# Feed-forward layers in three token blocks of 768, 384-column matmuls, one shared buffer for three sums of x

## Chip, cores and metric

The kernel runs on one core of a Trainium2 chip. The metric is the device time of one execution in microseconds (us). A core has TensorE (PE in the profile; PEld is its weight load), VectorE (DVE), ScalarE (ACT), GpSimd (POOL), and SyncE (SP), whose queue issues nearly all of this kernel's DMAs. Matmuls write the accumulator memory PSUM, the other engines work in the on-chip memory SBUF.

## What is computed

```python
scores = scale * q @ k^T                      # 4 batches, 8 heads, 576 tokens, 64 wide, causal
local = softmax(scores) @ v
mem_out = (phi(q) @ M_prev) / (phi(q) @ z_prev + 1e-6)
x = g * mem_out + (1 - g) * local             # 2304 tokens x 512
x = mish(x @ moe_w_in) @ moe_w_out            # 512 -> 2048 -> 512
out = silu(x @ moe2_w_in) @ moe2_w_out        # 512 -> 2048 -> 512
```

All is to float32 precision. The four weight matrices come as 64-bit floats and are turned into 32-bit ones on the chip.

## The kernel before

The attention stands first: 16 pairs of heads, each a list of some 70 steps (`pair_steps`, `Attn.steps`). Its result is left in SBUF as `xT`, features down the partitions and the 2304 tokens along. Then come two feed-forward layers (class `Moe`), phases 0 and 1.

A layer is cut into four groups of hidden columns (`NG`) and into token blocks. Before, there are four blocks of 512, 640, 512 and 640 tokens (`TBS` holds half of each, 256 and 320). One pass of a block through a group is a visit (`VISITS`): 32 visits in all. In odd groups the blocks are gone through backwards, so that the last block of a group is the first of the next.

The first product of a visit, x times w_in, is done as a 2 x 2 block product with seven instead of eight multiplications (`PRODUCTS`; numbered 1, 2, 6, 7, 5, 3, 4). Four of the seven take sums of x, called T1 to T4, three take parts of x itself (11, 21, 22). Each operand is split into a high and a low part (ACT rounds the high one, L984, DVE subtracts to get the low one, L977), so that a product is six matmuls of half a block's tokens (`product`, L1013 to L1015). A visit does this for two pairs of hidden chunks (c is 0 or 1): 84 matmuls. They go to the PSUM banks psX, psW and psY. ACT copies a bank out (L1044), DVE adds another to it (L1042), ACT applies Mish or Silu and rounds (L1048 to L1053), DVE takes the low part (L1054); the result is the tile `g`.

The second product, g times w_out (`out_part`, L1081), accumulates in the banks `acc`. In phase 0 the tokens are the columns: 512 of them in the small blocks, 320 twice in the large ones (`cuts`). In phase 1 a matmul always has the 512 output features as its columns. DVE adds `acc` to `xT` (L1102, ACT copies in the first group, L1100).

The split operands of x (seven tiles a block) are kept in two sets of buffers, one for even blocks and one for odd ones (`xop`: `tp % 2`). When a set goes to another block, the tiles are written to device memory once (`spill`, L991) and read back for later groups (`reload`, L995), on SP's queue.

The order in which every engine's instructions stand is computed when the kernel is built: `Steps.plan` plays all steps against a small table of durations and takes, on each engine, the ready step with the earliest due time. `SHIFT` adds a number to the due time of each class of steps; these numbers were sought by trial. A tile or a bank is handed on by `hold`: the first step of the next user waits for the last ones of the user before.

```python
for kc in range(2):
    nc.tensor.matmul(o, lhsT=W(0, kc), rhs=X(0, kc), ...)
    nc.tensor.matmul(o, lhsT=W(0, kc), rhs=X(1, kc), ...)
    nc.tensor.matmul(o, lhsT=W(1, kc), rhs=X(0, kc), ...)
```

Of the kernel before, what the change touches and what calls it, by code (L numbers as in the profile page):

```python
# [342 lines left out]
class Attn:  # L343
# [372 lines left out]
    def register(self, m):  # L716
# [8 lines left out]
        for p in range(B * NP):  # L725
# [213 lines left out]
class Moe:  # L939
    def __init__(self, tc, ctx, xT, weights, out):  # L940
        self.tc, self.nc, self.ctx = tc, tc.nc, ctx
        self.xT, self.w, self.out = xT, weights, out
        self.ps, self.pool = {}, {}
        self.dram = ctx.enter_context(tc.tile_pool(name="spill", bufs=1, space=bass.MemoryType.DRAM))
        self.x, self.g, self.sn, self.bank, self.acc, self.spilled = [{}, {}], {}, {}, {}, {}, {}

    def open(self, n):
# [23 lines left out]
    def splits(self, tp):
# [6 lines left out]
        home = {"T1": "11", "T3": "12", "T2": "22", "T4": "21"}  # L978
# [4 lines left out]
        for x in XOPS:  # L983
            f["h" + x] = lambda x=x: nc.scalar.copy(self.wide(tp, x, 0), B(home.get(x, x)))  # L984
            f["l" + x] = lambda x=x: sub(self.wide(tp, x, 1), B(home.get(x, x)), self.wide(tp, x, 0).bitcast(F32))
        return f

    def spill(self, ph, tp, x):
        t = self.x[tp % 2][x]
        d = self.spilled[ph, tp, x] = self.dram.tile([P, 4 * TBS[tp]], F32, name=f"sp{ph}{tp}{x}")  # L990
        self.nc.sync.dma_start(d, t.rearrange("p h n -> p (h n)").bitcast(F32))  # L991

    def reload(self, ph, tp, x):
        t = self.x[tp % 2][x]
        self.nc.sync.dma_start(t.rearrange("p h n -> p (h n)").bitcast(F32), self.spilled[ph, tp, x])  # L995

    def product(self, q, n):
# [13 lines left out]
        X = lambda h, kc: self.xop(tp, b, h)[:, kc * tb:(kc + 1) * tb]  # L1011
# [5 lines left out]
    def gt(self, q, c):  # L1017
        u = (q, c)
        if u not in self.g:
            k = (2 * (2 * q[0] + q[1]) + c) % 6  # L1020
            self.g[u] = self.pool[0 if k < 2 else 1].tile([P, 2, WIDE], F32R, tag=f"g{k}", name=f"g{k}")
        return self.g[u]

    def vt(self, q, c, h=None):
# [3 lines left out]
        tb = TBS[VISITS[q[0]][2]]  # L1028
        return self.sn[u][:, :2 * tb] if h is None else self.sn[u][:, h * tb:(h + 1) * tb]

    def fin(self, q):
        nc = self.nc
        ph, g, tp = VISITS[q[0]]
        tb = TBS[tp]
# [16 lines left out]
        hi = lambda c: self.gt(q, c)[:, 0, :2 * tb]  # L1051
        for c in range(2):
            f[f"h{c}"] = lambda c=c: nc.scalar.copy(hi(c), val(c))  # L1053
            f[f"l{c}"] = lambda c=c: nc.vector.tensor_tensor(  # L1054
                self.gt(q, c)[:, 1, :2 * tb], val(c), hi(c).bitcast(F32), op=ALU.subtract)
        return f

    def out_part(self, v, d, c):
        nc = self.nc
        ph, g, tp = VISITS[v]  # L1060
        tb = TBS[tp]
# [4 lines left out]
        for j in range(2):  # L1066
            w = self.w.W2[ph, g * GC + 2 * c + j]
            t = self.g[(v, c), j]
            if ph == 0:
                kc, hf = d  # L1070
                n = cuts(v)[0]
# [12 lines left out]
    def part(self, v, d):  # L1084
        ph, g, tp = VISITS[v]
        t0, tb = START[tp], TBS[tp]
        if ph == 0:
            n = cuts(v)[0]
# [3 lines left out]
        return self.xT[:, :, t0 + DM:t0 + DM + P]  # L1092

    def drain(self, v, d):
# [3 lines left out]
        acc = acc[:, :cuts(v)[0]] if ph == 0 else acc if d < KC else acc.rearrange("p (c n) -> p c n", c=KC)  # L1098
# [10 lines left out]
    def register(self, m, base, ends):  # L1109
        V = len(VISITS)  # L1110
        outs = lambda v: [(kc, h) for h in range(2 * TBS[VISITS[v][2]] // cuts(v)[0]) for kc in range(KC)] if (
            VISITS[v][0] == 0) else list(range(2 * TBS[VISITS[v][2]] // P))
        tb = lambda v: TBS[VISITS[v][2]]
        Q = lambda v, c, x: ("Q", (v, c), x)
        O = lambda v, d, c: ("O", (v, c), d)
        od = lambda v: 6 * sum(ff(n) for n in cuts(v))
        pd = lambda v: 6 * ff(tb(v))
# [3 lines left out]
        for v in range(V + 1):  # L1121
            for c in range(2):
# [14 lines left out]
        live = {}  # L1137
        run = []
        for v, (ph, g, tp) in enumerate(VISITS):
            b = tp % 2  # L1140
            if live.get(b, (None,))[0] != (ph, tp):
                live[b] = ((ph, tp), len(run))
                run.append([(ph, tp), [v], "comp" if g == 0 else "load"])
            else:
                run[live[b][1]][1].append(v)
        loaded = {r[0] for r in run if r[2] == "load"}
        ready = {}
        for n, ((ph, tp), vs, kind) in enumerate(run):
            b = tp % 2
            w = 2 * TBS[tp]  # L1150
            K = lambda x: ("X", (n, kind, ph, tp), x)
            users = {x: [Q(v, c, i) for v in vs for c in range(2) for i in PRODUCTS if PRODUCTS[i][1] == x] for x in XOPS}
            need = {x: due[Q(vs[0], 0, i)] for i in PRODUCTS for x in [PRODUCTS[i][1]]}
            if kind == "comp":
                f = self.splits(tp)
                pre = [f"open{b}"]
                if ph == 0:
                    t0 = START[tp]
                    pre += [(bb * NP + kc, e) for bb in range(t0 // S, (t0 + w - 1) // S + 1)
                            for kc in range(NP) for e in ends]  # L1160
                else:
                    pv = VISITS.index((0, NG - 1, tp))
                    pre += [("D", pv, d) for d in outs(pv)]
                D2, A1 = dve(w), sb1(w)
                mk = lambda x, e, d, deps, at: m.add(K(x), e, d, deps, f[x], at - 2.0)
                m.lock.update(K(x) for x in ["l" + x for x in XOPS] + ["T1", "T2", "T3", "T4"])
                mk("T1", "D", D2, [K("l11")], min(need["T1"], need["T2"]))
                mk("T3", "D", D2, [K("T1")], need["T3"])
                mk("T2", "D", D2, [K("T1"), K("T3"), K("l22")], need["T2"])
                mk("T4", "D", D2, [K("T2"), K("l21")], need["T4"])  # L1170
                for x in XOPS:
                    mk("h" + x, "A", A1, [K(x)] if x[0] == "T" else pre, need[x])
                    mk("l" + x, "D", D2, [K("h" + x)], need[x])
                    ready[n, x] = K("l" + x)
                firsts = {x: [K("h" + x)] for x in XOPS}
            else:
                for x in XOPS:
                    m.add(K(x), "S", w * 8 * P / 250e3 + 0.1, [("X", (spill[ph, tp], "comp", ph, tp), "sp" + x)],
                          lambda ph=ph, tp=tp, x=x: self.reload(ph, tp, x), need[x] - 4.0, lag=1.8)
                    ready[n, x] = K(x)  # L1180
                firsts = {x: [K(x)] for x in XOPS}
            lasts = dict(users)
            if kind == "comp" and (ph, tp) in loaded:
                if n == 0:
                    spill = {}
                spill[ph, tp] = n
                for x in XOPS:
                    m.add(K("sp" + x), "S", w * 8 * P / 250e3 + 0.1, [ready[n, x]],
                          lambda ph=ph, tp=tp, x=x: self.spill(ph, tp, x), need[x] + 20.0, lag=1.8)
                    lasts[x] = users[x] + [K("sp" + x)]  # L1190
            for x in XOPS:
                m.cap[f"X.{b}{x}"] = 1
                m.hold(f"X.{b}{x}", n, firsts[x], lasts[x], order=n)
            for v in vs:
                ready[v] = n
# [4 lines left out]
        for v, (ph, g, tp) in enumerate(VISITS):  # L1200
            w = TBS[tp]
            for c in range(2):
# [15 lines left out]
                gd = [f"open{int((2 * (2 * v + c) + j) % 6 >= 2)}" for j in range(2)]  # L1218
                for x, en, d, deps in (
# [4 lines left out]
                        ("h0", "A", sb1(2 * w), [N("m11"), N("m12"), gd[0]]), ("l0", "D", dve(2 * w), [N("h0")]),  # L1224
                        ("h1", "A", sb1(2 * w), [N("m2"), gd[1]]), ("l1", "D", dve(2 * w), [N("h1")])):
# [8 lines left out]
            comp = next(r for r in range(len(run)) if run[r][0] == (ph, tp) and run[r][2] == "comp")  # L1234
            split = [("X", (comp, "comp", ph, tp), "l" + x) for x in XOPS if x[0] == "T"]
            for d in outs(v):
                for c in range(2):
# [3 lines left out]
                          cols=(6 * cuts(v)[0], 6 * cuts(v)[0]))  # L1241
# [5 lines left out]
                n = cuts(v)[0]  # L1247
# [236 lines left out]
```

## Time and profile before

| what | value |
|---|---|
| median of 3 runs | 941.26 us (940.91 to 941.7) |
| the profiled execution | 941.86 us, its span from first to last instruction 940.1 us |
| PE busy | 918.7 us, 98% of the span |
| DVE, ACT, POOL busy | 651.8, 488.4, 144.0 us |
| granted TensorE clock | 0.999 of full speed |
| moved by DMA | 147.7 MB, mean 157 GB/s |

Matmuls are pipelined: the duration shown for one (0.28 us and more) is longer than its share of the engine, so the cost of a matmul in a stream is the distance from its start to the start of the next one. The chain of work that ended last lies 85% on PE, 8% on DVE and 3% on DMA.

### The profile page before, as it was taken

To read this page: it belongs to the slowest core of one execution; us is meant where nothing else is said; L and a number is where in the kernel's file an instruction comes from. 1 tells how busy PE (TensorE), PEld (TensorE's weight loads), DVE (VectorE), ACT (ScalarE), POOL (GpSimd) and SP (SyncE) were. 2 spreads that over 40 slices of the span, in tenths; PEclk is the share of its full clock that TensorE was granted. 3 is DMA by queue.
4 is the path that set the end of the run, shared out by engine and by line. 5 is a ranking of instruction groups with operands and counts; after the bars stand their busy time and mean duration, and the time that the engine had idled before them with its cause. 6 is when DMAs were issued, how large, how long until landed. Compare 5 with 4: busy or idle time off the path is not lost.

```text
span 940.1 us, 17127 instructions
## 1 busy us (share of the span) xinstructions
PE 918.7 (98%) x6544; PEld 811.0 (86%) x6544; DVE 651.8 (69%) x1444; ACT 488.4 (52%) x1150; POOL 144.0 (15%) x243
## 2 busy tenths in 40 slices
PE   6999999999999999999999999999999999999998
PEld 4676666899999999999999989898898888988986
DVE  5999989984896379535955899675457656743332
ACT  7899988775552354242441765564434343433421
POOL 7989998000000000000000000000000000000000
PEclk9999999999999999999999999999999999999999
DMA  6656554656466406630483646424541554034312
GB/s 234 203 179 208 157 174 128 241 236 241 151 195 225 135 1 198 223 111 1 146 272 115 256 189 240 157 90 160 186 144 45 165 188 135 1 99 171 140 68 79
DMA packets 60033, 147.72 MB, mean 157 GB/s; under 512 B 7600, under 2 KB 25136, under 8 KB 59952
## 3 DMA queue, kind: packets, MB, share of 16 engines
q1 hardware_dynamic: 59808, 146.30, 45.4%
q8 instruction: 52, 0.85, 0.4%
q10 hardware_dynamic: 144, 0.33, 0.1%
q14 instruction: 29, 0.24, 0.1%
HBM read 108.79 MB, written 37.81 MB: 156 GB/s over the span
## 4 chain that ended last, share of the span: by engine, by line
PE 85%; DVE 8%; DMA 3%; ACT 2%; issue 1%; POOL 1%; SPq 0%; DVEq 0%; ACTq 0%
PE acc L1081 42%; PE psX L1013 7%; PE psX L1014 7%; PE psX L1015 7%; PE psY L1013 4%; PE psY L1015 4%; PE psY L1014 4%; DVE sm L603 3%; PE ps_t L703 2%; PE ps_s L610 2%; PE psW L1014 2%; PE psW L1013 2%; PE psW L1015 2%; PE ps_t L501 1%; DVE h L494 1%
## 5 line engine op out<-in xcount | busy, mean ns | idle before, releaser
L1081 PE MATMUL acc<-g,w 128*128 128x320 f32 (+1 forms) x1152 | 210.4, 337 | 0.0
L1081 PE MATMUL acc<-w,g 128*128 128x512 f32 x864 | 208.6, 394 | 0.0
L1081 PEld LDWEIGHTS acc<-g,w 128*128 128x128 f32 x1152 | 184.4, 188 | 15.7 <-DVE g L1054 0.3
L1081 PEld LDWEIGHTS acc<-w,g 128*128 128x128 f32 x864 | 159.6, 188 | 33.9
L1102 DVE TENSOR_TENSOR xT<-acc,xT 128x512 f32<-128x512 f32 (+1 forms) x126 | 77.0, 612 | 91.9 <-PE acc L1081 91.7
L1044 ACT COPY vt<-psX 128x256 f32<-128x256 f32 (+1 forms) x192 | 73.4, 397 | 117.7 <-PE psX L1015 114.2
L1054 DVE TENSOR_TENSOR g<-vt,g 128x640 fp32r<-128x640 f32 (+1 forms) x128 | 93.9, 754 | 47.1 <-ACT g L1053 46.6
L1053 ACT CAST g<-vt 128x640 fp32r<-128x640 f32 (+1 forms) x128 | 83.4, 673 | 70.7 <-PE acc L1081 69.8
L1042 DVE TENSOR_TENSOR vt<-psY,vt 128x320 f32<-128x320 f32 (+1 forms) x128 | 58.1, 455 | 76.9 <-PE psY L1015 45.9
L1013 PE MATMUL psX<-x,w 128*128 128x320 f32 (+1 forms) x256 | 76.2, 298 | 0.1
L1014 PE MATMUL psX<-x,w 128*128 128x320 f32 (+1 forms) x256 | 75.7, 296 | 0.0
L1015 PE MATMUL psX<-x,w 128*128 128x320 f32 (+1 forms) x256 | 75.6, 295 | 0.0
L603 DVE CUSTOM_DVE_ANT_0 sm<-ps_s,mask 128x192 f32<-128x192 f32 (+3 forms) x128 | 66.7, 546 | 11.3 <-PE ps_s L610 9.8
L610 PE MATMUL ps_s<-kT,qT 64*128 64x288 f32 (+3 forms) x320 | 63.0, 482 | 10.0 <-DMA kT<-in_kT_dram 4.7
L1050 ACT ACTIVATE vt<-vt 128x512 f32<-128x512 f32 (+1 forms) x64 | 43.7, 685 | 33.3 <-DVE vt L1042 33.2
L1042 DVE TENSOR_TENSOR vt<-psW,vt 128x256 f32<-128x256 f32 (+1 forms) x64 | 29.0, 454 | 35.8 <-ACT vt L1044 18.6
L887 ACT CAST w<-val 128x512 fp32r<-128x512 f32 (+1 forms) x64 | 34.9, 566 | 36.4 <-DVE val L878 17.0
L610 PEld LDWEIGHTS ps_s<-kT,qT 64*128 64x128 f32 x320 | 30.1, 197 | 24.2 <-DVE m L603 10.9
L1013 PEld LDWEIGHTS psX<-x,w 128*128 128x128 f32 x256 | 48.3, 188 | 1.9 <-ACT vt L1044 0.4
L1014 PEld LDWEIGHTS psX<-x,w 128*128 128x128 f32 x256 | 48.3, 189 | 0.8
L1015 PEld LDWEIGHTS psX<-x,w 128*128 128x128 f32 x256 | 48.3, 189 | 0.0
L1049 ACT ACTIVATE vt<-psX 128x320 f32<-128x320 f32 (+1 forms) x64 | 26.2, 409 | 41.9 <-PE psX L1015 41.8
(124 smaller groups left out, 1987.4 us busy)
## 6 DMA issues: line engine op xcount, KB each, us to landing
stg<-in_moe_w_in_dram SPq DMA_DIRECT2D x32, 512.0 KB, 4.9
stg<-in_moe_w_out_dram SPq DMA_DIRECT2D x32, 512.0 KB, 4.1
x<-sp SPq DMA_DIRECT2D x18, 640.0 KB, 4.0
x<-sp SPq DMA_DIRECT2D x18, 512.0 KB, 5.2
sp<-x SPq DMA_DIRECT2D x12, 640.0 KB
sp<-x SPq DMA_DIRECT2D x12, 512.0 KB, 3.4
nv<-in_v_dram SPq DMA_DIRECT2D x16, 320.0 KB, 4.4
x1T<-sp01T SPq DMA_DIRECT2D x8, 640.0 KB, 4.7
```

Of the source, the lines that this page charges most:

```text
L603: nc.vector.tensor_tensor_reduce(out, ps, mask, -0.125, init, ALU.add, ALU.min, acc)
L610: nc.tensor.matmul(ps, lhsT=s["qT"][R[j], qcols(i)], rhs=s["kT"][R[j], k0 + cols.start:k0 + cols.stop], start=True, stop=True)
L1013: nc.tensor.matmul(o, lhsT=W(0, kc), rhs=X(0, kc), start=(n in (1, 2, 7) and kc == 0), stop=False, skip_group_check=True)
L1014: nc.tensor.matmul(o, lhsT=W(0, kc), rhs=X(1, kc), start=False, stop=False, skip_group_check=True)
L1015: nc.tensor.matmul(o, lhsT=W(1, kc), rhs=X(0, kc), start=False, stop=(kc == 1), skip_group_check=True)
L1042: nc.vector.tensor_tensor(o, self.bank[q, to], o, op=ALU.add)
L1044: f[f"s{n}"] = lambda n=n: nc.scalar.copy(val(*at[n]), self.bank[q, "X"])
L1050: f["m2"] = lambda: nc.scalar.activation(val(1), val(1), fn)
L1053: f[f"h{c}"] = lambda c=c: nc.scalar.copy(hi(c), val(c))
L1054: f[f"l{c}"] = lambda c=c: nc.vector.tensor_tensor(self.gt(q, c)[:, 1, :2 * tb], val(c), hi(c).bitcast(F32), op=ALU.subtract)
L1081: nc.tensor.matmul(y, lhsT=a, rhs=b, start=(c == 0 and k == 0), stop=(c == 1 and k == 5))
L1102: nc.vector.tensor_tensor(part, acc, part, op=ALU.add)
```

## The change

The tokens are cut into three blocks of 768 (`NB`, `TB` = 384, `WIDE` = 768), for 24 visits. Every matmul of the first product has 384 columns, and so has every matmul of the second product in phase 0 (`cut`); phase 1 keeps 512. The tiles of T1, T3 and T4 exist once and serve all blocks (`SHARED`, `home`); those of 11, 21, 22 and T2 still exist twice, the set taken by the parity of phase plus block. Spills and reloads are now decided for each tile apart. All `g` tiles lie in one pool. The numbers in `SHIFT` are all new, for the attention too.

```diff
-START = (0, 512, 1152, 1664)
-TBS = (256, 320, 256, 320)
-WIDE = 640
+NB = 3
+TB = NT // (2 * NB)
+WIDE = 2 * TB
+START = tuple(n * WIDE for n in range(NB))
 VISITS = [(ph, g, tp) for ph in range(2) for g in range(NG)
-          for tp in (range(4) if (g + ph) % 2 == 0 else range(3, -1, -1))]
+          for tp in (range(NB) if (g + ph) % 2 == 0 else range(NB - 1, -1, -1))]
+SHARED = {"T1": 0, "T3": 0, "T4": 1}
...
-def cuts(v):
-    return [DM] if VISITS[v][0] or TBS[VISITS[v][2]] * 2 == DM else [TBS[VISITS[v][2]]]
+def cut(v):
+    return DM if VISITS[v][0] else TB
+
+
+def home(ph, tp, x):
+    return x if x in SHARED else f"{(ph + tp) % 2}{x}"
...
-        w = TBS[n]
         for x in XOPS:
-            self.x[n][x] = pool.tile([P, 2, 2 * w], F32R, name=f"x{n}{x}")
+            if SHARED.get(x, n) == n:
+                k = x if x in SHARED else f"{n}{x}"
+                self.x[k] = pool.tile([P, 2, WIDE], F32R, name="x" + k)
...
-            self.g[u] = self.pool[0 if k < 2 else 1].tile([P, 2, WIDE], F32R, tag=f"g{k}", name=f"g{k}")
+            self.g[u] = self.pool[1].tile([P, 2, WIDE], F32R, tag=f"g{k}", name=f"g{k}")
...
+        runs = {}
         for v, (ph, g, tp) in enumerate(VISITS):
+            for x in XOPS:
+                rs = runs.setdefault(home(ph, tp, x), [])
+                if not rs or rs[-1][0] != (ph, tp):
+                    rs.append([(ph, tp), x, []])
+                rs[-1][2].append(v)
...
+                    if any(r[0] == (ph, tp) and r[2] != vs for r in rs):
+                        spills.add((ph, tp, x))
+                        users.append(K(ph, tp, "sp" + x))
+                else:
+                    first = ready[n, x] = ("X", ("load", ph, tp, n), x)
+                    m.add(first, "S", WIDE * 8 * P / 250e3 + 0.1, [K(ph, tp, "sp" + x)],
+                          lambda ph=ph, tp=tp, x=x: self.reload(ph, tp, x), need(n, x) - 4.0, lag=1.8)
...
 SHIFT = {
-    ('gate', 'exp'): -11714.19, ('gate', 'one'): -139.64, ('gate', 'sig'): -170.94, ('gate', 'rest'): -4059.43,
+    ('gate', 'exp'): 1927.87, ('gate', 'one'): -314.1, ('gate', 'sig'): 2556.39, ('gate', 'rest'): -16.76,
...
```

Line numbers move a little: L977 becomes L983, L984 L990, L991 L997, L995 L1001, L1013 to L1015 become L1018 to L1020, L1042 L1045, L1081 L1083.

PE, third group of phase 0. Tiles named xT_3295 (and x1T_3470 before) hold T3; w are split weights, g the activated hidden values. Before, this stands in the stretch in which the odd blocks' T3 goes from block 1 to block 3; each row of psX, psW or psY stands for the first of a product's six matmuls.

```order
L1013 MATMUL psY_5598<-x1T_3470,w_5162 128x320
L1013 MATMUL psW<-x_3466,w_5250 128x320
L1013 MATMUL psY_5665<-x0T_3295,w_5162 128x256
L1081 MATMUL acc<-g_5534,w_4517 128x512 x3
L1081 MATMUL acc<-g_5652,w_4517 128x320 x3
L1013 MATMUL psX<-x0T_3293,w_5162 128x256
L1013 MATMUL psY_5885<-x1T_3470,w_5162 128x320
```

With the change, the same group, T3 goes from block 0 to block 1:

```order
L1018 MATMUL psY_4962<-xT_3295,w_4916 128x384
L1018 MATMUL psW<-x_3291,w_4916 128x384
L1083 MATMUL acc<-g_4824,w_4571 128x384 x3
L1083 MATMUL acc<-g_4828,w_4513 128x384 x3
L1083 MATMUL acc<-g_4574,w_3800 128x384 x3
L1083 MATMUL acc<-g_4532,w_3836 128x384 x3
L1018 MATMUL psY_5036<-xT_3295,w_4696 128x384
```

Widths of 256, 320 and 512 have become 384, and between the last matmul on the old T3 and the first on the new one there are now 42 matmuls where there were 186.

DVE, first block of phase 0. The rows from x_3291 on are the splits of x (L977, now L983); val and stg belong to the weights, ps_t and W to the attention. Before:

```order
L977 TENSOR_TENSOR x_3291<-xT,x_3291 128x512
L977 TENSOR_TENSOR x_3292<-xT,x_3292 128x512
L494 COPY W_3272<-ps_t 128x2x4x64
L977 TENSOR_TENSOR x_3290<-xT,x_3290 128x512
L494 COPY h_3353<-ps_t 128x8x64
L977 TENSOR_TENSOR xT<-xT 128x2x256
L818 TENSOR_SCALAR val<-stg 128x512
L977 TENSOR_TENSOR xT<-xT 128x2x256
L977 TENSOR_TENSOR x0T_3293<-xT,x0T_3293 128x512
L977 TENSOR_TENSOR xT<-xT 128x2x256
L977 TENSOR_TENSOR x0T_3295<-xT,x0T_3295 128x512
```

With the change:

```order
L983 TENSOR_TENSOR x_3291<-xT,x_3291 128x768
L983 TENSOR_TENSOR x_3290<-xT,x_3290 128x768
L707 TENSOR_TENSOR xT<-ps_t,R 128x256
L494 COPY W_3272<-ps_t 128x2x4x64
L983 TENSOR_TENSOR xT<-xT 128x2x384
L983 TENSOR_TENSOR x_3292<-xT,x_3292 128x768
L983 TENSOR_TENSOR xT<-xT 128x2x384
L1045 TENSOR_TENSOR vt<-psW,vt 128x384
L983 TENSOR_TENSOR xT<-xT 128x2x384
L983 TENSOR_TENSOR xT_3295<-xT,xT_3295 128x768
L983 TENSOR_TENSOR xT_3293<-xT,xT_3293 128x768
L983 TENSOR_TENSOR x0T_3294<-xT,x0T_3294 128x768
```

The splits are half as wide again, and the low part of T3 (xT_3295) comes ninth after that of 21 (x_3291) instead of tenth.

SP, reloads of x for the third group of phase 0 and the visit after it. x_3290 to x_3292 are 11, 21 and 22, numbers 3293 to 3296 and 3446 the sums; sp are the copies in device memory. Before, for block 0:

```order
L995 DMA x0T_3295<-sp00T_3481 128x1024
L995 DMA x_3291<-sp_3344 128x1024
L995 DMA x_3290<-sp_3743 128x1024
L995 DMA x0T_3293<-sp00T_3399 128x1024
L995 DMA x_3292<-sp_3366 128x1024
L995 DMA x0T_3296<-sp00T_4028 128x1024
L995 DMA x0T_3294<-sp00T_3429 128x1024
```

With the change, for blocks 1 and 2 of the third group:

```order
L1001 DMA x_3290<-sp_3965 128x1536
L1001 DMA xT_3295<-sp01T_3563 128x1536
L1001 DMA x_3291<-sp_3470 128x1536
L814 DMA stg<-in_moe_w_in_dram 128x4x256 x2
L1001 DMA x0T_3294<-sp02T_3784 128x1536
L1001 DMA xT_3293<-sp01T_3931 128x1536
L1001 DMA x_3292<-sp_3662 128x1536
L1001 DMA xT_3446<-sp01T_3715 128x1536
L1001 DMA xT_3295<-sp02T_3753 128x1536
L1001 DMA xT_3293<-sp02T_4035 128x1536
L1001 DMA xT_3446<-sp02T_3858 128x1536
```

A reload is of 768 KB instead of 512 or 640, those of two blocks stand interleaved, and T1, T3 and T4 (3293, 3295, 3446) go through the same three tiles twice in a row.

## Rows read from the trace of the kernel before

**Rows 1.** The page: the span, and PE's busy time with its instructions.

```profile
span 940.1 us, 17127 instructions
PE 918.7 (98%) x6544; PEld 811.0 (86%) x6544; DVE 651.8 (69%) x1444; ACT 488.4 (52%) x1150; POOL 144.0 (15%) x243
```

**Rows 2.** Busy time by stretch: span, busy and count of each engine, granted clock, DMA.

```profile
20.00:160.00 140.00, 133.23 (x1634) 90.79 (x1632) 135.02 (x432) 128.07 (x401) 125.02 (x205) 1.00 0.54 171
160.00:180.00 20.00, 17.98 (x194) 14.95 (x189) 18.79 (x39) 14.08 (x32) 4.55 (x8) 1.00 0.70 239
180.00:540.00 360.00, 360.00 (x2369) 344.71 (x2369) 249.38 (x481) 167.55 (x345) 1.29 (x1) 1.00 0.48 169
540.00:560.00 20.00, 18.87 (x116) 17.18 (x115) 19.58 (x40) 12.62 (x23) 0.00 (x0) 1.00 0.48 192
```

**Rows 3.** Waits, whole span: engine and line, releaser, us in total, times, longest.

```profile
DVE xT L1102 <- PE acc L1081: 91.7, 61, 5.5
```

**Rows 4.** Timeline of PE and DVE: gaps at the first feed-forward matmuls and at 542 us.

```profile
167.28 0.39 PE L1013 MATMUL psW<-x,w 128*128 128x256 f32 x1
168.74 0.76 PE L703 MATMUL ps_t<-W,nv 128*64 128x320 f32 x4 [0.39 <-ACT h L491]
172.02 0.39 PE L1013 MATMUL psX<-x,w 128*128 128x256 f32 x1
...
176.48 0.39 PE L1013 MATMUL psX<-x0T,w 128*128 128x256 f32 x1 [0.46 <-ACT vt L1044]
...
542.10 0.41 PE L1015 MATMUL psY<-x1T,w 128*128 128x320 f32 x1 [1.01 <-DVE w L878]
```

**Rows 5.** Groups of PE by line and shape: xcount, busy us, mean ns, idle before.

```profile
L1081 PE MATMUL acc<-w,g 128*128 128x512 f32 x864 | 208.6, 394 | 0.0
L1081 PE MATMUL acc<-g,w 128*128 128x320 f32 x768 | 118.5, 309 | 0.0
L1081 PE MATMUL acc<-g,w 128*128 128x512 f32 x384 | 93.3, 395 | 0.0
L1013 PE MATMUL psX<-x1T,w 128*128 128x320 f32 x128 | 39.9, 312 | 0.0
...
L1013 PE MATMUL psX<-x0T,w 128*128 128x256 f32 x128 | 36.4, 285 | 0.5 <-ACT vt L1044 0.5
```

**Rows 6.** Timeline of PE: start, duration; first and last of streams of one width.

```profile
753.04 0.28 PE L1013 MATMUL psX<-x0T,w 128*128 128x256 f32 x1
...
756.50 0.28 PE L1015 MATMUL psY<-x0T,w 128*128 128x256 f32 x1
...
188.19 0.31 PE L1013 MATMUL psY<-x1T,w 128*128 128x320 f32 x1
...
196.85 0.31 PE L1015 MATMUL psX<-x1T,w 128*128 128x320 f32 x1
...
639.99 11.32 PE L1081 MATMUL acc<-w,g 128*128 128x512 f32 x48
651.15 0.28 PE L1013 MATMUL psX<-x0T,w 128*128 128x256 f32 x1
```

**Rows 7.** Timeline of DVE: two splits of 512 columns, one behind the other.

```profile
171.29 0.68 DVE L977 TENSOR_TENSOR x0T<-xT,x0T 128x512 fp32r<-128x512 f32 x1
171.90 0.68 DVE L977 TENSOR_TENSOR xT<-xT 128x512 f32<-128x512 f32 x1
```

**Rows 8.** DMA issues: xcount, KB each, median us to landing; last row, from 395 to 402 us.

```profile
x1T<-sp13T SPq DMA_DIRECT2D x8, 640.0 KB, 5.5
...
x0T<-sp00T SPq DMA_DIRECT2D x8, 512.0 KB, 7.5
...
x<-sp SPq DMA_DIRECT2D x1, 640.0 KB, 3.5
```

**Rows 9.** Timeline, end of the span: last drain, last store.

```profile
935.64 0.69 DVE L1102 TENSOR_TENSOR xT<-acc,xT 128x512 f32<-128x512 f32 x1 [2.08 <-PE acc L1081]
936.36 0.58 SPq L1107 DMA_DIRECT2D out_dram<-xT  x1
```

More of the change, by code (lines that the diff above doesn't have):

```diff
@@ L1070, in out_part @@
                 kc, hf = d
-                n = cuts(v)[0]
+                n = cut(v)
                 s = slice(kc * P, (kc + 1) * P)
@@ L1110, in register @@
         V = len(VISITS)
-        outs = lambda v: [(kc, h) for h in range(2 * TBS[VISITS[v][2]] // cuts(v)[0]) for kc in range(KC)] if (
-            VISITS[v][0] == 0) else list(range(2 * TBS[VISITS[v][2]] // P))
-        tb = lambda v: TBS[VISITS[v][2]]
+        outs = lambda v: list(range(WIDE // P)) if VISITS[v][0] else [(kc, h) for h in range(2) for kc in range(KC)]
         Q = lambda v, c, x: ("Q", (v, c), x)
         O = lambda v, d, c: ("O", (v, c), d)
-        od = lambda v: 6 * sum(ff(n) for n in cuts(v))
-        pd = lambda v: 6 * ff(tb(v))
+        od = lambda v: 6 * ff(cut(v))
+        pd = 6 * ff(TB)
         t, due, begin = base, {}, {}
@@ L1147, in register @@
[L1147 to L1190, printed above, removed]
-            for x in XOPS:
[L1192 to L1195, printed above, removed]
@@ new lines, in register @@
+            for x in XOPS:
[3 more added lines that the diff above has]
+                rs[-1][2].append(v)
+        need = lambda v, x: due[Q(v, 0, next(i for i in PRODUCTS if PRODUCTS[i][1] == x))]
+        K = lambda ph, tp, x: ("X", ("comp", ph, tp), x)
+        ready = {}
+        spills = set()
+        for k, rs in runs.items():
+            m.cap["X." + k] = 1
+            for (ph, tp), x, vs in rs:
+                users = [Q(v, c, i) for v in vs for c in range(2) for i in PRODUCTS if PRODUCTS[i][1] == x]
+                n = vs[0]
+                if VISITS[n][1] == 0:
+                    first, ready[n, x] = K(ph, tp, "h" + x), K(ph, tp, "l" + x)
+                    if any(r[0] == (ph, tp) and r[2] != vs for r in rs):
[5 more added lines that the diff above has]
+                          lambda ph=ph, tp=tp, x=x: self.reload(ph, tp, x), need(n, x) - 4.0, lag=1.8)
+                for v in vs:
+                    ready[v, x] = ready[n, x]
+                m.hold("X." + k, n, [first], users, order=n)
@@ L1217, in register @@
                 e = due[N(4)] + 4.0
-                gd = [f"open{int((2 * (2 * v + c) + j) % 6 >= 2)}" for j in range(2)]
+                gd = "open1"
                 for x, en, d, deps in (
@@ L1233, in register @@
                     m.hold(f"M.g{(2 * n + j) % 6}", (q, j), [N(f"h{j}")], [O(v, d, c) for d in outs(v)], order=n)
-            comp = next(r for r in range(len(run)) if run[r][0] == (ph, tp) and run[r][2] == "comp")
-            split = [("X", (comp, "comp", ph, tp), "l" + x) for x in XOPS if x[0] == "T"]
+            split = [K(ph, tp, "l" + x) for x in XOPS if x[0] == "T"]
             for d in outs(v):
```

104 lines of the change are left out of this document (58 added, 46 removed), and 190 rows, old and new, of the table SHIFT.

## The prediction

> **What bounds the kernel now.** I read the page first: the span is 940.1 us and PE is busy for 918.7 us of it [rows 1]. A share over the whole span mixes stages, so I read the busy time by stretch next [rows 2]. From 20 to 160 us, the attention, DVE is the fullest engine (135.0 of 140 us). From 180 to 540 us PE is busy for 360.00 of 360.00 us: in the feed-forwards nothing but the number and the pace of the matmuls sets the time. The waits say the same from the other side: DVE waits 91.7 us in all for the banks that PE has still to finish [rows 3]. The few places where PE stands still are its first 10 us on the feed-forwards and the end of phase 0; the timeline has the gaps, 0.39, 0.46 and 1.01 us [rows 4].
>
> So the feed-forwards can be added up. The groups of PE by shape give the counts [rows 5]: of the second product 384 matmuls of 512 columns, 768 of 320 and, in phase 1, 864 of 512; of the first product 1344 of 256 and 1344 of 320 (84 in each of 16 visits; the view cuts them into groups of 64 and 128, of which two stand there). The duration shown is not the price, since matmuls overlap. The price is the distance of starts in an unbroken stream [rows 6]: 256 columns (756.50 - 753.04) / 29 = 119.3 ns, 320 columns (196.85 - 188.19) / 59 = 146.8 ns, 512 columns (651.15 - 639.99) / 48 = 232.5 ns. Sum of the part that the change touches: 160.3 + 197.3 + 112.7 + 89.3 = 559.6 us; phase 1's second product adds 200.9, together 760.5 us. From the first feed-forward matmul (167.28) to the last drain (935.64) there are 768.4 us. The 7.9 us left over are 3.3 us of the attention's own last matmuls (168.74 to 172.02 [rows 4]) and some 4.6 us of gaps, of which the three shown make 1.9.
>
> **The change, part by part.**
>
> *Width of the matmuls.* 3840 matmuls of 256, 320 and 512 columns become 24 x 84 + 12 x 96 = 3168 of 384; the columns in sum stay the same, and 672 matmuls fall away. The granted clock is 1.00 throughout [rows 2], the level of 2.4 GHz, at which the columns alone take 106.7, 133.3 and 213.3 ns. So a matmul costs 12.6, 13.5 and 19.2 ns more than its columns [rows 6]. A width of 384 is in no row. From below: 160.0 ns for its columns and the 13.5 ns of width 320 are 173.5 ns, and 3168 of them 549.6 us, a gain of 10.0. From above: the straight line from 256 to 512 gives 175.9 ns, 557.3 us, a gain of 2.3. The line from 320 to 512, the nearest rows, gives 175.2; a curve through all three lies a little below it, since the excess rises faster at the wide end. I take 175.0 ns: 554.4 us, **-5.2 us**. This lies on PE, which has no cover in this stage, so it counts in full.
>
> The Trainium skill, "TensorE: Matmul & The Clock Gate", section "Back-to-back issue gap", gives a warm isolated matmul N / 2.4 + 2.5 ns and says that sustained streams run closer together still (131 ns at 512 columns). The rows disagree with both figures: 232.5 ns at 512 columns, and 12.6 to 19.2 ns over the columns instead of 2.5. By its fixed 2.5 ns the 672 matmuls would be worth an estimated 1.7 us.
>
> *Start of the feed-forwards.* Splits of x get half as wide again. Two of 512 columns start 0.61 us apart [rows 7]; 768 columns lie between that and 0.61 x 1.5 = 0.92, nearest the latter. The low part of T3 comes ninth after that of 21, not tenth: 8.2 us against 6.1, up to 2.1 later. PE comes to it after four products of six matmuls and the attention's 3.3 us: 24 x 0.175 + 3.3 = 7.5 us against 24 x 0.119 + 3.3 = 6.2, so 1.3 later. A new gap of up to 0.8 us may stand there, against that of 0.46 at 176.48 [rows 4]. Against it, the new order has two or three weight and attention instructions of DVE fewer ahead of the first split. At some 0.6 us each they bring the first product forward, because DVE bounds the attention. I take **-0.5 us** for the two together, and keep -2.5 to +2.5, four instructions of 0.61 us either way.
>
> *Other gaps.* With 24 visits instead of 32 there are fewer changes of block and of bank. The gap of 1.01 us at 542.10 hangs on the order at the end of phase 0, which is new. I take **-0.5 us**; the bounds are -1.9 (all three gaps shown vanish) and +3.0 (three more of the longest).
>
> *Shared T1, T3 and T4, and the traffic.* A reload of such a tile can be issued only once PE has left the old block's copy. The wait stands on SP; behind it stand more reloads and the weight loads of later groups. In the new order 12 reloads have no more than 36 to 42 matmuls between the last use of the old copy and the first of the new, 6.3 to 7.4 us at 175 ns; the other windows are longer, five of them under 9.6 us. A reload of 640 KB with no other in front lands 3.5 us after issue; a group of eight of that size has a median of 5.5 us, and the slowest group, of 512 KB, one of 7.5 [rows 8]. For 768 KB, by size, 3.5 x 1.2 = 4.2 and 5.5 x 1.2 = 6.6 us. The upper one just fits, so I cost it at nothing: the cover is PE's other products, and it is gone when issue to landing exceeds about 6.9 us. The bounds are 0 and +53 us (7.5 x 1.5 = 11.25 us, 4.4 too late, 12 times). I stay near the low one, since the reloads are 60 of 768 KB (46 MB) in place of 42 of 640 and 42 of 512 (48 MB), the spills fall from 32 to 26 MB, and DMA is busy half the time [rows 2].
>
> *End and the other engines.* The order at the end is the same: last drain at 935.64, last store issued at 936.36 [rows 9], nothing gained. DVE and ACT lose about a hundred instructions each; they wait for PE in this stage [rows 3], so this costs and brings nothing.
>
> **Sum:** -5.2 - 0.5 - 0.5 = -6.2 us. The profiled execution took 941.86 us, 0.6 above the median of 941.26; from it 935.7, from the median **935.1 us**.
>
> **Rivals.** (A) The forecast, 931.5 to 938.5.
> (B) A matmul has a fixed cost and nothing that grows with width beyond the line: 175.9 ns, so -2.3 and the two small terms, 938.0 us. For it speaks that 256 to 320 rises by only 0.9 ns; against it, that 512 lies 5 ns above that. The rule of the Trainium skill named above ("TensorE: Matmul & The Clock Gate", "Back-to-back issue gap") is of this kind too; the trace does not bear its size out.
> (C) The other side: the shared T tiles come late. With 8.0 us from the last use to landing (the slowest median, 7.5, and half a microsecond for the larger tile), each of the 12 short windows (6.9 us in the mean) leaves PE idle for 1.1 us: +14, about 949 us. It decides from 7.5 us on: 12 x 0.68 = 8.1 us eats the gain and the bound below. Against it: the 4.2 and 6.6 us that the other rows give by size.
> (D) The attention, whose order is new throughout, ends 3 to 6 us later, since DVE is the bound there with 5 us to spare in 140 [rows 2]: 938 to 941 us.
> (E) The width costs least (173.5 ns) or the gaps go: 929 to 931 us.
> That the change does not do what it says is excluded by the order, in which all these matmuls have 384 columns.
>
> **How the numbers follow.** Chances: A 0.58, B 0.08, C 0.10, D 0.12, E 0.12. A measurement of this kernel tells 0.2%, 1.9 us, from no change: faster ends at 939.4, slower begins at 943.1. Faster: A but for 0.02, B but for 0.02, E, and 0.04 of D, together 0.78. Slower: 0.08 of C and 0.01 of D, 0.09. The rest, 0.13, is within. The range from 930.0 to 941.0 leaves out C, 0.04 of E and 0.03 of D, 0.17 in all.
>
> **What would show it.** In the trace after: the distance of starts in a stream of 384 columns (175.0 ns; over 175.9 or under 173.5 breaks the first term); the first feed-forward matmul at about 166.8 us instead of 167.28 (later than 169 is D); no gaps of PE that end on a reload of T1, T3 or T4 (a row of waits with several such, each over 0.5 us, is C); 360 of 360 us busy in the middle; the last drain some 6 us earlier, with the same end behind it.

## The result and the profile after

The changed kernel takes 933.47 us (median of 4 runs, 933.2 to 933.79) against 941.4 of the kernel before on the same chip: ratio 0.9916, 95% interval 0.9899 to 0.9934. That is 7.9 us faster, where 6.2 were forecast. The profiled execution took 933.48 us. The sum came out near, but three of its terms did not: the rows below take it apart.

The page of the kernel after, span and busy time, answers to [rows 1]:

```profile
span 931.7 us, 15347 instructions
PE 916.0 (98%) x5872; PEld 825.7 (89%) x5872; DVE 639.3 (69%) x1342; ACT 469.7 (50%) x1006; POOL 144.6 (16%) x243
```

The span is 8.4 us shorter; PE's share is the same 98%. By stretch, with the columns of [rows 2]:

```profile
20.00:160.00 140.00, 135.35 (x1671) 93.59 (x1671) 137.46 (x440) 130.13 (x405) 126.57 (x210) 1.00 0.58 174
160.00:180.00 20.00, 19.39 (x157) 16.11 (x154) 19.50 (x29) 15.19 (x28) 3.54 (x4) 1.00 0.68 250
180.00:540.00 360.00, 360.00 (x2051) 360.00 (x2050) 248.68 (x452) 160.88 (x281) 1.45 (x1) 1.00 0.46 157
540.00:560.00 20.00, 20.00 (x116) 20.00 (x115) 18.82 (x31) 10.59 (x16) 0.00 (x0) 1.00 0.24 79
```

PE is still full in the middle. It is now full from 540 to 560 us as well (18.87 before). In the attention's 140 us DVE is busy for 137.46 us instead of 135.02 and does 440 instructions instead of 432. The timeline of PE at the start, where [rows 4] showed three gaps:

```profile
164.33 0.44 PE L1018 MATMUL psW<-x,w 128*128 128x384 f32 x1
...
167.65 0.76 PE L703 MATMUL ps_t<-W,nv 128*64 128x320 f32 x4
168.24 0.82 PE L703 MATMUL ps_t<-h,nv 128*64 128x256 f32 x8
...
170.93 0.44 PE L1018 MATMUL psW<-x,w 128*128 128x384 f32 x1
...
176.12 0.44 PE L1018 MATMUL psX<-xT,w 128*128 128x384 f32 x1 [0.57 <-ACT vt L1047]
```

The first feed-forward matmul comes at 164.33 us instead of 167.28. From 164.33 to 167.65 there now stand 18 feed-forward matmuls ahead of the attention's last ones, where there were 6; and those last ones begin 1.1 us earlier. In these rows one gap is left, 0.57 us on the bank's copy.

The groups of the second product, with the columns of [rows 5], and then streams of one width in PE's timeline, as [rows 6]:

```profile
L1083 PE MATMUL acc<-g,w 128*128 128x384 f32 x1152 | 213.3, 338 | 0.0
L1083 PE MATMUL acc<-w,g 128*128 128x512 f32 x864 | 211.3, 395 | 0.0
```

```profile
300.04 0.33 PE L1018 MATMUL psX<-x,w 128*128 128x384 f32 x1
...
304.72 0.33 PE L1018 MATMUL psY<-xT,w 128*128 128x384 f32 x1
...
316.32 8.61 PE L1083 MATMUL acc<-g,w 128*128 128x384 f32 x48
324.77 0.34 PE L1018 MATMUL psX<-x0T,w 128*128 128x384 f32 x1
...
663.37 7.17 PE L1083 MATMUL acc<-w,g 128*128 128x512 f32 x30
670.38 0.34 PE L1018 MATMUL psX<-x0T,w 128*128 128x384 f32 x1
```

Here is something new: one width has two paces. In the first product 27 matmuls of 384 go by in 4.68 us, 173.3 ns each; in the second 48 of the same width take 8.45 us, 176.0 ns each, with the granted clock at 1.00 in both. And 512 columns, which the change leaves alone, take (670.38 - 663.37) / 30 = 233.7 ns, where the row before gave 232.5.

The whole of the feed-forwards, from all distances of starts on PE (a distance over 20 ns above the median of its width counts as a gap, with what it has above the median):

| part | before, us | after, us | change | forecast |
|---|---|---|---|---|
| first feed-forward matmul | 167.28 | 164.33 | -2.95 | -0.5 |
| changed matmuls, without gaps | 559.5 | 556.8 | -2.7 | -5.2 |
| gaps of PE from there on | 4.8 | 1.3 | -3.5 | -0.5 |
| 512 columns of phase 1 | 200.3 | 201.2 | +0.9 | 0 |
| last matmul to the end of the span | 4.9 | 4.8 | -0.1 | 0 |

Together that is -8.4 us. The shared T tiles cost nothing. No gap of PE ends on a reload, although the shortest time from issue to first use is only 6.1 us. The timeline of SP and PE shows one such, and the DMA issues of 358.5 to 365 us the landing:

```profile
358.64 0.34 SPq L1001 DMA_DIRECT2D xT<-sp01T  x1
...
364.78 0.34 PE L1018 MATMUL psX<-xT,w 128*128 128x384 f32 x1
```

```profile
xT<-sp01T SPq DMA_DIRECT2D x2, 768.0 KB, 4.6
```

Issued at 358.64, landed 4.6 us later, used at 364.78: 1.5 us to spare. Over the whole span the medians of such groups are 4.4 to 7.9 us, against 5.5 and 7.5 in [rows 8]; the slow ones stand where 13 us or more are left.

### The profile page after: what moved, and what is told of

It is laid out like the page before. It is cut to its first block, busy times and chain, and to the rows that moved or that the text cites. A ratio compares the mean times of both kernels' runs of the same rounds, so it can differ in the third digit from the quotient of the medians.

```text
span 931.7 us, 15347 instructions
## 1 busy us (share of the span) xinstructions
PE 916.0 (98%) x5872; PEld 825.7 (89%) x5872; DVE 639.3 (69%) x1342; ACT 469.7 (50%) x1006; POOL 144.6 (16%) x243
## 4 chain that ended last, share of the span: by engine, by line
PE 88%; DVE 7%; POOL 2%; issue 1%; ACT 1%; DMA 1%; DVEq 0%; SPq 0%; ACTq 0%; POOLq 0%
PE acc L1083 43%; PE psX L1018 7%; PE psX L1020 7%; PE psX L1019 7%; PE psY L1020 4%; PE psY L1018 4%; PE psY L1019 4%; PE ps_s L610 3%; DVE sm L603 3%; PE ps_t L703 2%; PE psW L1018 2%; PE psW L1020 2%; PE psW L1019 2%; PE ps_t L501 2%; DVE h L494 1%
## 5 line engine op out<-in xcount | busy, mean ns | idle before, releaser
L1083 PE MATMUL acc<-g,w 128*128 128x384 f32 x1152 | 213.3, 338 | 0.0
L1083 PE MATMUL acc<-w,g 128*128 128x512 f32 x864 | 211.3, 395 | 0.0
L1083 PEld LDWEIGHTS acc<-g,w 128*128 128x128 f32 x1152 | 203.7, 188 | 0.0
L1083 PEld LDWEIGHTS acc<-w,g 128*128 128x128 f32 x864 | 161.6, 188 | 33.6 <-DVE xT L1105 0.2
L1105 DVE TENSOR_TENSOR xT<-acc,xT 128x384 f32<-128x384 f32 (+1 forms) x126 | 76.4, 610 | 93.7 <-PE acc L1083 93.5
L1056 ACT CAST g<-vt 128x768 fp32r<-128x768 f32 x96 | 76.8, 833 | 117.5 <-PE acc L1083 117.1
L1057 DVE TENSOR_TENSOR g<-vt,g 128x768 fp32r<-128x768 f32 x96 | 89.5, 953 | 64.5 <-ACT g L1056 64.5
L1045 DVE TENSOR_TENSOR vt<-psY,vt 128x384 f32<-128x384 f32 x96 | 53.1, 555 | 101.3 <-ACT vt L1047 55.4
L1047 ACT COPY vt<-psX 128x384 f32<-128x384 f32 x144 | 68.6, 479 | 96.7 <-PE psX L1020 84.7
L603 DVE CUSTOM_DVE_ANT_0 sm<-ps_s,mask 128x448 f32<-128x448 f32 (+3 forms) x128 | 65.9, 541 | 11.4 <-PE ps_s L610 9.3
L1018 PE MATMUL psX<-x,w 128*128 128x384 f32 x192 | 64.8, 337 | 0.0
L1018 PE MATMUL psY<-xT,w 128*128 128x384 f32 x192 | 64.8, 337 | 0.0
L1020 PE MATMUL psY<-xT,w 128*128 128x384 f32 x192 | 64.7, 337 | 0.0
L1019 PE MATMUL psX<-x,w 128*128 128x384 f32 x192 | 64.7, 337 | 0.0
L1019 PE MATMUL psY<-xT,w 128*128 128x384 f32 x192 | 64.7, 337 | 0.0
L1020 PE MATMUL psX<-x,w 128*128 128x384 f32 x192 | 64.7, 337 | 0.0
L628 ACT ACTIVATE Ph<-sm,m 128x448 f32<-128x448 f32 (+1 forms) x64 | 45.7, 718 | 0.5 <-DVE m L603 0.4
```

What stands on the lines that cost most here:

```text
L603: nc.vector.tensor_tensor_reduce(out, ps, mask, -0.125, init, ALU.add, ALU.min, acc)
L628: nc.scalar.activation(ptile(i)[:, o:o + w] if i else G("P0")[:, 2], s[f"sm{i}{j}"], AF.Exp, bias=s[f"m{i}"][:, j:j + 1], scale=-1.0, accu ...
L1018: nc.tensor.matmul(o, lhsT=W(0, kc), rhs=X(0, kc), start=(n in (1, 2, 7) and kc == 0), stop=False, skip_group_check=True)
L1019: nc.tensor.matmul(o, lhsT=W(0, kc), rhs=X(1, kc), start=False, stop=False, skip_group_check=True)
L1020: nc.tensor.matmul(o, lhsT=W(1, kc), rhs=X(0, kc), start=False, stop=(kc == 1), skip_group_check=True)
L1045: nc.vector.tensor_tensor(o, self.bank[q, to], o, op=ALU.add)
```

## The experiments

The built program gives each tile its address in SBUF. Put beside the trace, matmul by matmul, the two paces follow the addresses. In the kernel before and after, the pools that grow from the upper end of SBUF start 32 bytes off a multiple of 64, those from the lower end on a multiple. In the trace after, matmuls of 384 whose moving operand and whose successor's weights had the same address modulo 64 took 174.7 ns, the others 176.5; for 512 it was 230.9 and 233.6. The theory called P in the expectations came from this. Below, the distance of two operands is the difference of their start addresses; a layout is uniform when all distances are 0 modulo 128, otherwise mixed.

**A pad of 32 bytes at the upper end**, which moves all tiles there by 32:

```diff
+    pad = ctx.enter_context(tc.tile_pool(name="pad", bufs=1, side="right"))
+    pad.tile([P, 8], F32, name="pad")
     big = ctx.enter_context(tc.tile_pool(name="big", bufs=1))
```

> The changed kernel with 32 bytes set aside at the upper end of SBUF: all feed-forward operands then start at multiples of 64 bytes, where x of the odd set, T4 and all g stood 32 bytes off. Theory P (pairing): a matmul's pace depends on whether its moving operand and the next matmul's weights have the same address modulo 64. In the trace after, unpaired matmuls of 384 take 176.5 ns and paired ones 174.7, unpaired ones of 512 take 233.6 and paired 230.9; 1875 and 685 are unpaired, so 1875 x 1.8 + 685 x 2.7 ns = 5.2 us less, 928 us. Rival (the pace goes with the tile or the time of the run, not with the address): 933 to 934 us, means unchanged at 176.2 and 233.2 ns.

Measured: 928.24 us, ratio to before 0.9867 (0.9852 to 0.9881). The time is the one expected, the split of it is not: the second product's 384 columns fell from 176.3 to 174.1 ns and the first product's from 175.5 to 174.4, but 512 only from 233.2 to 232.8, not to 230.9. Its streams:

```profile
314.23 8.56 PE L1083 MATMUL acc<-g,w 128*128 128x384 f32 x48
322.63 0.33 PE L1018 MATMUL psX<-x0T,w 128*128 128x384 f32 x1
...
658.78 7.17 PE L1083 MATMUL acc<-w,g 128*128 128x512 f32 x30
665.78 0.34 PE L1018 MATMUL psX<-x0T,w 128*128 128x384 f32 x1
```

These are 175.0 ns for 384 columns (176.0 without the pad) and still 233.3 for 512.

**The same 32 bytes at the lower end** (`side="left"`):

> The changed kernel with 32 bytes set aside at the lower end instead: every feed-forward operand then starts 32 bytes behind a multiple of 64. Theory P (pairing) has all operands paired and expects the time of the pad at the upper end, 928 us. Rival (a start at a multiple of 64 is what is fast): all matmuls of 384 at 176.5 ns or more and of 512 at 233.6 or more, 936 us or more.

Measured: 928.15 us, 0.9866 (0.9849 to 0.9882), with the same mean paces as the pad above to 0.02 ns. Both pads change the distance between the two ends by the same 32 bytes. So what counts is where operands lie to each other, not a start at a multiple of 64.

**The pad of 32 in the kernel before:**

> The kernel before with 32 bytes set aside at the upper end, so that all its feed-forward operands stand at multiples of 64 bytes too. Theory P: 1763 unpaired matmuls of 320 lose 1.0 to 1.5 ns each and 730 of 512 lose 2.9 ns, 3.9 to 4.8 us less, 937 us. Against it the changed kernel with the same pad shows what the width of the matmuls is worth without this effect: 174.6 ns a matmul of 384 would make the first term 5.5 us again. Rival: no change, 941 us.

Measured: 941.06 us, 1.0003 (0.9994 to 1.0013): nothing. 320 columns went from 147.0 to 146.7 ns, 256 from 119.1 to 119.4, 512 from 232.2 to 232.1. P falls. A pad of 32 turns distances of 32 and 96 into 64, not into 0, if one counts modulo 128; sorted that way, 384 columns ran at 173.3 to 173.5 ns at a distance of 64 and 512 columns at 233.2. This is P2, which the next three test.

**A pad of 96 at the upper end** (`pad.tile([P, 24], ...)`), distances 0 modulo 128 everywhere:

> The changed kernel with 96 instead of 32 bytes set aside at the upper end: the moving operand of every feed-forward matmul and the weights of the next one then have the same address modulo 128, where the pad of 32 left 1875 matmuls of 384 and 685 of 512 at a distance of 64. Theory P (only the distance modulo 64 counts): 928.2 us, as with 32. Theory P2 (the distance modulo 128 counts, and differently by width; with the pads of 32, 384 columns took 173.3 to 173.5 ns at 64 and 175.2 at 0, 512 columns 233.2 at 64 and 231.4 at 0): 1875 x 1.8 = +3.4, 685 x 1.8 = -1.2, about 930.4 us.

Measured: **922.93 us**, 0.9803 (0.9786 to 0.982), better than either theory allowed. The page's span:

```profile
span 921.5 us, 15347 instructions
```

The streams in PE's timeline:

```profile
314.69 8.48 PE L1083 MATMUL acc<-g,w 128*128 128x384 f32 x48
323.01 0.33 PE L1018 MATMUL psX<-x0T,w 128*128 128x384 f32 x1
...
657.17 7.00 PE L1083 MATMUL acc<-w,g 128*128 128x512 f32 x30
664.02 0.33 PE L1018 MATMUL psX<-x0T,w 128*128 128x384 f32 x1
```

384 columns take 173.3 ns and 512 take 228.3: the fast pace, and for 512 one that no distance had shown in the mean of a mixed layout (230.4 at best).

**The same in the kernel before:**

> The kernel before with 96 bytes set aside at the upper end: all distances 0 modulo 128 (before: 730 of 512 columns and 1763 of 320 at 32 or 96; with 32 bytes they stood at 64 and nothing changed). Theory P2: 730 x 2.5 ns (233.4 to 230.9) = 1.8 us and 1763 x 0.5 ns (147.0 to 146.5) = 0.9 us less, about 938.3 us. Theory P, which the pad of 32 already contradicts in this kernel, and a rival by which the old block sizes have nothing to gain from addresses: 940.8 to 941.1 us.

Measured: 936.62 us, 0.9953 (0.9939 to 0.9967), 4.4 us better, where P2 said 2.8. 512 columns went from 232.2 to 228.2 ns:

```profile
637.54 11.07 PE L1081 MATMUL acc<-w,g 128*128 128x512 f32 x48
648.45 0.28 PE L1013 MATMUL psX<-x0T,w 128*128 128x256 f32 x1
```

That is 227.3 ns, at the place where [rows 6] gave 232.5. Widths 256 and 320 hardly moved (119.1 to 119.5, 147.0 to 146.6).

**32 bytes above and 64 below the even set of x**, most first products at a distance of 64:

```diff
+        if n == 0:
+            pool.tile([P, 16], F32, name="pad0")
         for x in XOPS:
             if SHARED.get(x, n) == n:
```

> The changed kernel with 32 bytes at the upper end and 64 bytes between the weights and the even set of x at the lower side: 1943 of the 2016 matmuls of the first product and 876 of 1152 of the second then stand at a distance of 64 modulo 128 from the next weights, against 868 and 1007 with the 32 bytes alone. Theory P2: 1075 x 1.9 ns = 2.0 us less, 131 more matmuls at 0 cost 0.2 back, 162 of 512 gain 0.3: about 926.1 us. Theory P: 928.2 us.

Measured: 926.51 us, 0.984 (0.9821 to 0.9859), where P2 said 926.1. It was right here, since the layout is again a mixed one, like those that its prices came from; it was wrong for the two uniform ones. A price taken from a mixed layout does not hold for a uniform one.

**All operands 64 bytes behind a multiple of 128** (32 bytes at the upper end, 64 at the lower):

> The changed kernel with 32 bytes at the upper end and 64 bytes at the lower end: every feed-forward operand starts 64 bytes behind a multiple of 128, so all distances are 0 modulo 128, as with the 96 bytes at the upper end (922.9 us), but no address is a multiple of 128. Theory P3 (what counts is that all operands have the same address modulo 128, whatever it is): 922.9 us, within 1; 384 columns 173.3 to 173.8 ns, 512 columns 229.0. Rival A (a start at a multiple of 128 is what is fast): 926 us or more. Rival B (the class means of the mixed layouts hold: 175.2 and 231.4 ns at a distance of 0): about 930 us, which the 96 bytes already contradict.

Measured: **922.67 us**, 0.9796 (0.9769 to 0.9823); 173.3 and 173.8 ns for 384 columns in the second and first product, 229.05 for 512, the same as the pad of 96 to 0.02 ns. So P3 stands in all that was run: 512 columns are fastest when all their operands in SBUF share one address modulo 128, at either of the two that were tried (0 and 64); 384 columns are as fast then as they were at a distance of 64 in the mixed layouts (173.3 to 173.5). Which reads get in each other's way is not shown: only addresses were moved, and with them those of tiles that other engines and the DMAs read and write.

**The reloads of T issued twice:**

```diff
         self.nc.sync.dma_start(t.rearrange("p h n -> p (h n)").bitcast(F32), self.spilled[ph, tp, x])
+        if x in SHARED:
+            self.nc.sync.dma_start(t.rearrange("p h n -> p (h n)").bitcast(F32), self.spilled[ph, tp, x])
```

> The changed kernel with each reload of T1, T3 and T4 issued twice (the same bytes to the same tile). Cover theory: a reload lands 4.4 us after issue and has 6.3 to 7.4 us in the 12 shortest windows, so the single one is hidden with 2 us to spare and the double one, 7.5 to 9 us, is not: PE waits 1 to 2.5 us in each of the 12, +12 to +30 us, 945 to 963 us, and the waits name the reloads. Rival (the cover is larger than the order says, or transfers run side by side): within 1 us of 933.5.

Measured: 997.52 us (one run), 64 us more than the changed kernel, twice the upper end of what was expected. The timeline of SP, that of PE, and the view by core with the mean granted clock:

```profile
409.40 0.32 SPq L1001 DMA_DIRECT2D xT<-sp02T  x1
414.76 0.32 SPq L1003 DMA_DIRECT2D xT<-sp02T  x1
415.17 0.38 SPq L1001 DMA_DIRECT2D xT<-sp02T  x1
420.96 0.32 SPq L1003 DMA_DIRECT2D xT<-sp02T  x1
```

```profile
418.93 0.69 PE L1020 MATMUL psX<-xT,w 128*128 128x384 f32 x1 [3.25 <-DMA xT<-sp02T]
419.42 0.52 PE L1021 MATMUL psX<-xT,w 128*128 128x384 f32 x1
419.74 0.52 PE L1022 MATMUL psX<-xT,w 128*128 128x384 f32 x1
```

```profile
core 0: 995.7 us, clock 0.978
```

The second reload waits on SP until the first has landed (409.40 to 414.76), and the next tile's reload stands behind it. So not only the 12 short windows were missed: PE waited for reloads in 21 places, and these gaps sum to 47 us. Most of the rest, 14 us, are 92 matmuls at half pace: after this gap they start 0.32 us apart (419.42 to 419.74), which is the level of 1.2 GHz for 384 columns. The granted clock is 0.50 from 419.0 to 421.6 us and 0.978 in the mean of the execution. The cover theory holds, its price was far too low.

**The old numbers in the new blocks** (the table `SHIFT` of the kernel before in the changed kernel):

> The changed kernel (blocks of 768, shared tiles) with the numbers of SHIFT from the kernel before, those for the attention included; numbers for reloads of T that did not exist there fall to zero. Theory O (the 3 us at the start and the end of the phase 0 stalls come from the new order, not from the blocks): the first feed-forward matmul comes at 166.3 us or later, instead of 164.3, gaps of PE come back after 165 us, 936 to 945 us. Rival (the blocks bring them): first feed-forward matmul at 164 to 165 us and about 934 us. Either way the stream of 384 columns stays at 174 to 177 ns.

Measured: 949.86 us (one run). The first feed-forward matmul comes at 165.5 us, between the two theories. Gaps come back: counted as in the table above they are 16.4 us in 54 places, where the changed kernel has 1.3 us in 7. Nine waits make 10.4 us of it, and 25 matmuls 0.32 us apart 3.6 (the granted clock is 0.50 from 182 to 187 us). In PE's timeline the first row here is the longest wait, the other two stand where phase 0 ends, as the gap of 1.01 us in [rows 4] did:

```profile
181.71 0.69 PE L1018 MATMUL psX<-xT,w 128*128 128x384 f32 x1 [3.10 <-ACT vt L1047]
...
551.55 0.44 PE L1018 MATMUL psW<-x,w 128*128 128x384 f32 x1 [1.32 <-ACT w L893]
552.96 0.69 PE L1020 MATMUL psW<-x,w 128*128 128x384 f32 x1 [0.80 <-DVE w L884]
```

The streams of 384 columns keep their pace (175.4 and 176.3 ns), so the order alone makes the difference to the changed kernel: 15.1 us of gaps and 1.2 us of a later start. That old numbers do not fit new blocks is part of this, so the 949.86 is not the price of the blocks alone.

**The new numbers in the old blocks:**

> The kernel before (blocks of 512 and 640, no shared tiles) with the numbers of SHIFT from the change. In its order 481 instruction rows of DVE stand ahead of the first split of x, as in the change, against 484 in the kernel before and in the changed kernel with the old numbers, where that split began at 166.8 and 165.2 us. Theory O (the earlier start of the feed-forwards is the new numbers' doing): first split at 162 to 164 us, as in the change (162.9). Rival (the blocks or their layout bring it): 165 us or later. The feed-forwards get an order that was not sought for them, so their gaps and the time are left open: 938 to 955 us.

Measured: 942.91 us (one run). DVE's first split of x, here, in the changed kernel, and in the run with the old numbers:

```profile
161.85 1.29 DVE L977 TENSOR_TENSOR x<-xT,x 128x512 fp32r<-128x512 f32 x2 [0.31 <-ACT x L984]
```

```profile
162.88 1.83 DVE L983 TENSOR_TENSOR x<-xT,x 128x768 fp32r<-128x768 f32 x2
```

```profile
165.24 1.83 DVE L983 TENSOR_TENSOR x<-xT,x 128x768 fp32r<-128x768 f32 x2 [0.39 <-ACT x L990]
```

With the new numbers the split begins at 161.6 to 162.9 us in all eight profiles, in old blocks or new; with the old ones at 165.2 to 166.8 in four. The earlier start is the doing of the numbers, as far as one run of each exchange can show it. The smaller gaps are not theirs alone: in this run the gaps are 10.1 us in 54 places, against 4.8 in 33 in the kernel before, and eat the earlier start (162.98 instead of 167.28 us for the first feed-forward matmul). Each table has more gaps in the other's blocks than in its own; which part of the 3.5 us of gaps the blocks saved and which the numbers is not shown.

A kernel with all of T1 to T4 twice was not tried: three more tiles of 6 KB a partition do not fit beside the others. Nor was one with the first two g tiles at the lower end, as before: there is no room for them while the attention still holds its upper tiles.

## Why the prediction was right, and where it was not

*Width of the matmuls: right in sign, mis-sized.* The term was -5.2 us at 175.0 ns; it measured -2.7 at 175.8 in the mean (175.5 in the first product, 176.3 in the second). That is inside its bounds, 173.5 to 175.9, at the upper end. What failed is the step that read 119.3, 146.8 and 232.5 ns as prices of widths. The 232.5 was a mean over layouts of 230.5 to 233.7, and at one address modulo 128 512 columns take 228.2 to 229.0. At that layout 384 takes 173.3 to 173.8 ns, which is about the lower bound taken from the row of width 320 (160.0 + 13.5). The curve that was to lie under the line had its bend from the 232.5. (The line from 320 to 512 gives 175.4 at 384, not 175.2; the sum does not rest on it.) With the same layout on both sides the width is worth 558.0 - 550.0 = 8.0 us, and the two kernels lie 936.62 - 922.93 = 13.7 us apart. The change as it stands gives much of this back: all g tiles moved to the upper end, so 1007 of the second product's 1152 matmuls of 384 columns, and 836 of the first's, stand at a distance of 96 bytes. The same is why phase 1, costed at nothing, lost 0.9 us: 685 of its 864 matmuls are at another distance than 0 modulo 128, where 491 were.

*Start of the feed-forwards: right in sign, mis-sized.* It was -0.5 with bounds of 2.5 either way; it came to -2.95, beyond the bound. In both kernels 1808 of the attention's 1840 matmuls stand ahead of the first feed-forward one; what shrank is the time that PE waits between 20 us and that matmul, from 7.9 to 4.7 us. The step counted the instructions of DVE ahead of the first split (481 instead of 484, some 0.6 us each) and left out the time in which DVE itself stands still: from 80 us to the first feed-forward matmul that was 4.3 us before, and 0.3 us with the new numbers. This start also moves from one execution to the next: 166.4 to 167.3 us in three profiles with the old blocks and numbers, 163.0 to 164.3 in seven with the new ones. The feared 0.8 us at T3 did not come: the gap at 176.12 is 0.57, where 0.46 stood.

*Other gaps: mis-sized.* -0.5 against -3.5. The bound of -1.9 counted the three gaps that stood in the rows. The kernel before had 33 distances over 20 ns too long, 4.8 us in all. The three gaps make 2.3 us of them by the distance of starts (1.9 by the idle time that the rows show), one more 0.3, and 29 are of 0.02 to 0.11 us each, 2.2 us together. Some of these stand behind a wait: the matmul there is followed by the next one 0.10 us later than usual, at 256 columns as at 384. Before, and with the change:

```profile
176.48 0.39 PE L1013 MATMUL psX<-x0T,w 128*128 128x256 f32 x1 [0.46 <-ACT vt L1044]
176.70 0.28 PE L1014 MATMUL psX<-x0T,w 128*128 128x256 f32 x1
176.82 0.28 PE L1015 MATMUL psX<-x0T,w 128*128 128x256 f32 x1
```

```profile
176.12 0.44 PE L1018 MATMUL psX<-xT,w 128*128 128x384 f32 x1 [0.57 <-ACT vt L1047]
176.40 0.34 PE L1019 MATMUL psX<-xT,w 128*128 128x384 f32 x1
176.57 0.34 PE L1020 MATMUL psX<-xT,w 128*128 128x384 f32 x1
```

The granted clock is 1.00 in this stretch, so this is not the half pace of the doubled reloads. Part of the waits went because 18 instead of 6 feed-forward matmuls now stand ahead of the attention's last ones, where PE waited 0.39 us at 168.74. The small ones were in the 4.6 us that the prediction's own sum left over; it only did not ask how much of that could go.

*Shared tiles: right.* Costed at nothing. The two landings that the trace has in short windows took 4.4 and 4.6 us, near the lower of the two estimates (4.2 and 6.6). Rival C was a real danger and its price was too low: a doubled reload takes some 9.5 us (issued at 409.40, used at 418.93), for which the sum of rival C (12 windows, each with 6.9 us of cover) gives 31 us. It cost 64, since a late reload also delays those behind it on SP, and behind gaps such as that of 3.25 us PE goes at half pace for a while.

*Rivals B and D.* B, 175.9 ns, comes close to the pace measured (175.8) by luck, since its line ends at the 232.5. Its rule fares better than its number: with all addresses equal the line from 256 (119.5) to 512 columns (228.2) gives 173.9 ns at 384, where 173.3 to 173.8 were measured. So most of the rise of the excess over the columns (12.6 to 19.2 ns from 256 to 512 columns) came from the addresses; with all of them equal it goes from 12.8 to 14.9. D did not come: the attention ended earlier, not later. *End and other engines: right*, last matmul to end 4.8 us against 4.9.

So the total lay only 1.6 us below the forecast (2.2 in the profiled executions) because two misses of 2.5 and 3.0 us to one side and two of 2.5 and 0.9 us to the other partly cancelled. The range held; the sum was luckier than its terms.

## What to carry to other kernels

Before you price an instruction by its pace, look at how that pace scatters within one shape: two values at one width and one clock are a sign that something other than the width is in the price. Where PE is full, compare the addresses of all operands modulo 128: setting aside 96 bytes was worth 10.5 us (933.47 to 922.93), more than this whole change. When an order is sought anew, price the sum of all small gaps as its upper bound, not the two or three that stand out.

## What was not expected of the hardware

TensorE's pace depends on how its operands lie in SBUF. With one granted clock and nothing else changed, 512 columns took 229.0 ns where all operands had the same address modulo 128 and 232.4 to 233.7 ns (means over hundreds of matmuls of one kernel) where the moving operand and the next weights were 32, 64 or 96 bytes apart; 384 columns took 173.3 ns and, 96 bytes apart, 176.5, but at 64 bytes no more than 173.5. The work was the same in all. In the means of whole kernels the effect at 320 columns and below is 0.4 ns or less, and at 256 not even of the same sign. The distance of these two operands does not settle the pace by itself: at a distance of 0 within mixed layouts 512 columns still took 230.4 to 231.6 ns.

The Trainium skill, "TensorE: Matmul & The Clock Gate", section "Step-by-step: what each phase is for", says that TensorE reads the moving operand and the weights through two independent ports, so that loading the next weights takes nothing from the running matmul. The runs differ from that here, by up to 4.6 ns in 233.7, if it is these two reads that meet; that it is them was not shown. The same page of the Trainium skill, section "Back-to-back issue gap", gives an isolated matmul 2.5 ns over its columns. The best stream of 384 columns here has 13.3, and no layout came near 2.5.
